# Two seven-product pairs in block 1 of a linear-attention and GEGLU kernel, and k-v of batch 1 on column halves

## The chip, the cores and the metric

The kernel runs on one core of a Trainium2 chip. The metric is the device time of one execution in microseconds (us), as the median of five runs. The engines are TensorE (PE, with its weight loads PEld), VectorE (DVE), ScalarE (ACT), GpSimd (POOL) and SyncE (SP), which issues nearly all of the transfers.

## The reference

For q, k and v of 8 batches, 8 heads, 576 positions and 64 values per head, it computes a linear attention: a softmax of q over the 64 values, a softmax of k over the 576 positions, kv = k-softmax transposed times v (64 x 64 per head), and x = q-softmax times kv. With the heads side by side, x is a matrix of 4608 rows and 512 columns. Then comes a GEGLU layer with 1536 inner columns:

```
kv  = einsum('bhsd,bhse->bhde', softmax(k, axis=2), v)
x   = einsum('bhsd,bhde->bhse', softmax(q, axis=-1), kv)   # -> [4608, 512]
g   = x @ w_gate
out = (0.5 * g * (1 + erf(g / sqrt(2))) * (x @ w_val)) @ w_out
```

## The kernel before, in words

**Blocks.** The work goes by batches. Each of the 8 batches has 512 main positions, which make one block of the layer; the 64 remaining positions of all batches make a ninth block, which is run before the last batch. While TensorE does the layer of batch b, the other engines prepare the attention of batch b + 1 and load batch b + 2 or so. There is no scheduler: every instruction stands where the program calls it, and side work is hung on places in the block with `at(b, kind, place, functions)` and called by `ride`. The kinds are FI (behind an inner tile of a block that is done tile by tile), PR (a letter in a written list of steps) and NS (places in the output stage).

**The layer, tile by tile.** The 1536 inner columns are 12 tiles of 128, numbered 0 to 11. A tile in its plain form is 4 matmuls of 512 columns for the gate (bank psg) and 4 for the value (psv), line 467. `gate` (line 470) then takes the Gelu on ScalarE into gl and multiplies on VectorE into ht, the inner activations. Blocks 0 and 1 do all twelve tiles like this. Their first tiles are interleaved with the end of the attention (`ffn_first0`, `ffn_first`), since the four parts of x arrive one by one.

**The layer, by seven products.** From block 2 on, the tiles k and k + 3 (k = 0, 1, 2, and 6, 7, 8 in some blocks) can be done as a pair by Strassen's seven products of half size instead of eight. `pair_step` (line 630) has four steps, written "k.1" to "k.4" in the lists: step 1 does products 1 and 5, step 2 products 6 and 3, step 3 products 7 and 2, step 4 product 4. Each product is 4 matmuls of 256 columns (line 606), so a pair is 28. In between, ScalarE copies bank pga to pgb and takes snapshots (snq), VectorE adds them into a tile cc or into the idle eq buffer of odd batches (cc_b), ScalarE takes the Gelu of cc, and GpSimd multiplies its halves into ht (`upper`, line 653). It needs sums of the weights (`sum_wgv`, tiles ws and, in place, wg_sb and wv_sb) and four sums of x (`sum_x`, GpSimd, line 593, tile xs). The lists THREE (block 2), FOUR and SIX (lines 611 to 616) give the order of the steps; "6g" and "6v" are the gate and the value half of plain tile 6 (`half`, line 620), the letters are places for side work.

**The output.** Blocks from 1 on use seven products again in `out_strassen` (line 728): products 1, 2, 5, 6, 3, 7, 4 of 12 matmuls each (line 718), in banks psa, psb, psc. They need sums of ht (`sum_h`, line 566: s1 and s2 in sh, one in place in ht, one in s4) and of the output weights (`sum_w`, line 552, tiles tw). In block 1 all of the ht sums are on VectorE, in steps of two neighbouring tiles (SUMS, line 706); in later blocks a part of them is on GpSimd, in steps of tiles j, j + 3, j + 6 and j + 9.

**The attention.** `exp` (line 208, ScalarE) makes eq and ek; `norm` or `norm_pair` (lines 235 and 253) reduce on VectorE and multiply on GpSimd or VectorE; `cast_v` (line 217) casts v on GpSimd; k-v is `unit_kv` for batch 1 (`kv_mm`, line 279: 10 matmuls of 130 columns for two head pairs, of which the mask keeps the diagonal blocks) and `unit_kv4` from batch 2 on (line 336: 40 matmuls of 65 columns, two heads on the two column halves). q is transposed by TensorE for batches 0 and 1, and by one transfer for batch 2 on (`unit_td`, line 383, issued by SyncE). `unit_x` and `unit_x4` make x. ek and v have one buffer each, eq has two.

**Places around the change.** In block 1 the eq of batch 2 is normalized behind tiles 2 to 4 (tile numbers 0-based), the first half of its k is exponentiated behind tile 4, its v is cast behind tile 5 and its q transposed behind tile 8. The second half of k and the q of batch 3 are exponentiated behind tile 11, the k of batch 3 in the output stage after `unit_kv4` of batch 2; there v of batch 3 is loaded and cast too. `unit_x4` of batch 2 comes before the last product, and then `one_ring` joins the two banks kept for the attention (att_ring) with the other six.

## Time and profile before

| | us |
|---|---|
| median of five runs | 293.68 (293.62 to 293.84) |
| the profiled execution | 293.66 |
| its span in the profile | 291.9 |
| TensorE busy | 282.5 |
| VectorE busy | 222.2 |
| GpSimd busy | 200.5 |
| ScalarE busy | 194.9 |
| block 1 on TensorE, first matmul of its first tile to the first of block 2 | 48.59 to 81.73 |
| output stage of block 1 | 70.76 to 81.73 |
| block 2 to its output stage | 81.73 to 101.27 |

The clock granted to TensorE was full over the whole span. In the views of the profile, a row of the order of work gives the start in us from the start of the span, the duration in us, the engine, the line of the program, the operation, what it writes from what it reads, the shape, how many instructions are merged in the row, and in brackets the idle time before it with the releaser. Matmul rows overlap at their ends, as each matmul is shown until its result is out. "PE pskv L343" is TensorE's write to tile pskv at line 343. SPq is SyncE's queue, whose rows show how long the queue was held by issuing, not how long a transfer took.

### The profile page before, as it was taken

The numbers are of one execution on the slowest core, as the hardware profiler recorded it, in microseconds if no ns is written. First come the engines' busy times: TensorE is split into PE (matmuls) and PEld (weight loads), VectorE is DVE, ScalarE is ACT, GpSimd is POOL, SyncE is SP. The second block draws the span as 40 slices with busy tenths as digits, with TensorE's granted clock in tenths as the row PEclk, the third lists the DMA queues.
The fourth block names the chain that finished last, engine by engine and source line by source line (L and its number), as shares of the span: only waits on it lengthen the run. The fifth ranks groups of instructions, "written<-read, shape, count | busy, mean of one in ns | idle before, by whom it ended". The sixth has DMA issues, their size and how long they took to land.

```text
span 291.9 us, 6352 instructions
## 1 busy us (share of the span) xinstructions
PE 282.5 (97%) x2449; PEld 203.0 (70%) x2449; DVE 222.2 (76%) x412; ACT 194.9 (67%) x322; POOL 200.5 (69%) x187
## 2 busy tenths in 40 slices
PE   3999999999999999999999999999999999999994
PEld 1444445445866687778776878687868888888883
DVE  2954889878878768677967797687868879938992
ACT  3763367785786578758986798669864577537650
POOL 1557746970489799877888688869895576283640
PEclk9999999999999999999999999999999999999999
DMA  6999999998059704990299119901141110033003
GB/s 216 374 381 387 401 392 390 357 342 236 5 183 380 158 3 144 352 225 3 116 313 277 36 74 325 323 3 74 73 78 25 72 74 0 3 72 75 0 2 144
DMA packets 54622, 51.72 MB, mean 177 GB/s; under 512 B 18496, under 2 KB 50496, under 8 KB 54592
## 3 DMA queue, kind: packets, MB, share of 16 engines
q1 hardware_dynamic: 52864, 49.49, 53.9%
q10 hardware_dynamic: 1728, 1.84, 1.9%
q8 instruction: 19, 0.31, 0.5%
q14 instruction: 11, 0.09, 0.1%
HBM read 37.75 MB, written 9.44 MB: 162 GB/s over the span
## 4 chain that ended last, share of the span: by engine, by line
PE 94%; DVE 2%; DMA 2%; ACT 0%; issue 0%; ACTq 0%
PE pga L606 19%; PE psa L718 15%; PE psg L467 14%; PE psv L467 14%; PE pgc L606 9%; PE psc L718 7%; PE pgb L606 5%; PE psb L718 4%; PE psy L535 4%; DMA qt<-in_q_dram 2%; PE pskv L343 2%; PE psx L430 1%; DVE rq L240 1%; PE psx L409 1%; DVE eq L250 0%; PE pskv L284 0%
## 5 line engine op out<-in xcount | busy, mean ns | idle before, releaser
L467 PE MATMUL psg<-xt,wg_sb 128*128 128x512 f16 x184 | 49.3, 379 | 0.0
L467 PE MATMUL psv<-xt,wv_sb 128*128 128x512 f16 x184 | 49.2, 379 | 0.0
L250 POOL TENSOR_TENSOR eq<-eq,rrq 128x640 f16<-128x640 f16 (+1 forms) x27 | 34.7, 1305 | 11.6 <-DVE rrq L242 8.1
L718 PEld LDWEIGHTS <-ht 128*128 128x128 f16 x384 | 36.6, 98 | 7.6 <-issue 2.5
L606 PEld LDWEIGHTS <-wv_sb 128*128 128x128 f16 x248 | 24.1, 98 | 9.4 <-issue 1.0
L467 PEld LDWEIGHTS <-wv_sb 128*128 128x128 f16 x184 | 17.9, 98 | 18.0 <-issue 0.2
L653 POOL TENSOR_TENSOR ht<-eq 128x512 f16<-128x512 f32 x14 | 17.8, 1272 | 18.0 <-ACT eq L651 18.0
L467 PEld LDWEIGHTS <-wg_sb 128*128 128x128 f16 x184 | 18.0, 98 | 16.5
L576 POOL TENSOR_TENSOR s<-ht,sh 128x512 f16<-128x512 f16 x19 | 22.4, 1178 | 9.8 <-DVE sh L576 9.8
L634 DVE SCALAR_TENSOR_TENSOR ht<-pga,glq 128x256 f16<-128x256 f32 x31 | 13.1, 421 | 20.7 <-ACT glq L633 20.6
L188 POOL CAST v<-vt 128x640 f16<-128x640 f32 x26 | 18.8, 763 | 12.8 <-PE pskv L343 11.3
L576 POOL TENSOR_TENSOR ht<-ht 128x512 f16<-128x512 f16 x19 | 23.1, 1216 | 6.1 <-DVE sh L576 6.1
L606 PEld LDWEIGHTS <-wg_sb 128*128 128x128 f16 x248 | 24.2, 98 | 2.8
L653 POOL TENSOR_TENSOR ht<-cc 128x512 f16<-128x512 f32 x15 | 19.5, 1302 | 8.5 <-ACT cc L651 8.5
L472 ACT ACTIVATE gl<-psg 128x512 f32<-128x512 f32 x24 | 13.8, 598 | 16.6 <-PE psg L467 16.5
L633 ACT ACTIVATE glq<-pgb 128x256 f32<-128x256 f32 x31 | 11.7, 379 | 18.7 <-PE pgb L606 10.9
L718 PE MATMUL psa<-tw,ht 128*128 128x256 f16 x192 | 23.4, 272 | 0.1
L473 DVE SCALAR_TENSOR_TENSOR ht<-psv,gl 128x512 f16<-128x512 f32 x24 | 16.1, 686 | 9.3 <-PE psv L467 7.4
L212 ACT ACTIVATE ek<-kt 128x1280 f16<-128x1280 f32 (+1 forms) x11 | 19.1, 1748 | 5.5 <-DMA kt<-in_k_dram 4.0
L663 ACT COPY pgb<-pga 128x512 f32<-128x512 f32 x31 | 18.0, 580 | 6.7 <-PE pga L606 6.4
L643 ACT ACTIVATE snq<-pga 128x512 f32<-128x512 f32 x31 | 18.5, 599 | 4.0 <-PE pga L606 3.7
L240 DVE TENSOR_REDUCE rq<-eq 128x20 f32<-128x1280 f16 (+1 forms) x12 | 17.2, 1431 | 4.5 <-ACT eq L212 4.5
(172 smaller groups left out, 729.2 us busy)
## 6 DMA issues: line engine op xcount, KB each, us to landing
out_dram<-yo SPq DMA_DIRECT2D x15, 512.0 KB, 3.4
kt<-in_k_dram SPq DMA_DIRECT2D x7, 640.0 KB, 9.5
vt<-in_v_dram SPq DMA_DIRECT2D x7, 640.0 KB, 5.6
qt<-in_q_dram SPq DMA_DIRECT2D x7, 640.0 KB, 8.1
qt<-in_q_dram SPq DMA_DIRECT2D x8, 512.0 KB, 8.2
wost<-in_moe_w_out_dram SPq DMA_DIRECT2D x6, 512.0 KB, 7.9
kt<-in_k_dram SPq DMA_DIRECT2D x6, 512.0 KB, 9.3
vt<-in_v_dram SPq DMA_DIRECT2D x6, 512.0 KB, 6.0
```

The source lines that it names most:

```text
L188: nc.gpsimd.tensor_copy(out=dst, in_=src)
L212: nc.scalar.activation(out=dst[:, n0:NC, h0 * D:h1 * D].rearrange(o, d=D, **({"t": 2} if b >= QUAD else {})), in_=heads(tiles[(nm, b)], b, ...
L240: nc.vector.reduce_sum(rq, e, axis=mybir.AxisListType.X)
L250: (nc.gpsimd if eng == "pool" else nc.vector).tensor_tensor(out=e, in0=e, in1=rrq.unsqueeze(-1).to_broadcast((P, n, 2, D)), op=ALU.mult)
L467: nc.tensor.matmul(ps, w[:, ci, fi * P:(fi + 1) * P], xt[:, ci, :], start=(ci == 0), stop=(ci == HP - 1))
L473: nc.vector.scalar_tensor_tensor(out=ht[:, fi, :], in0=psv, scalar=_H_SCALE, in1=gl, op0=ALU.mult, op1=ALU.mult)
L576: (nc.gpsimd if eng == "pool" else nc.vector).tensor_tensor(out=o, in0=a, in1=b, op=op)
L606: nc.tensor.matmul(ps[:, t], a, x, start=(first and t == 0 and c == 0), stop=(c == 1), skip_group_check=True)
L643: nc.scalar.activation(out=sn, in_=ps, func=ACTF.Copy, scale=_H_SCALE)
L653: (nc.vector if k == NFI - NO // 2 - 1 else nc.gpsimd).tensor_tensor(out=ht[:, k:k + NO // 2 + 1:NO // 2, 256:512], in0=cc[:, :, 0], in1=c ...
L663: nc.scalar.copy(out=pb, in_=pa)
L718: nc.tensor.matmul(ps[t], a, w, start=(first and j == js[0] and (t == ts[0] or ps[t].tensor is not ps[ts[0]].tensor)), stop=(j == js[-1]), ...
```

## The change

Block 1 gets a list of steps of its own, TWO. Its first three tiles, interleaved with the end of the attention, are now 6, 7 and 8; then come tile 9, two pairs in turns (0 with 3, 1 with 4), and tiles 10, 11, 2 and 5 in the plain form. The sums of x of batch 1 and the normalization of batch 2 in pairs go behind tile 8; the second of the two rings is joined right after the first three tiles. The weight sums that pairs 0 and 1 need in place of wg_sb and wv_sb (`sum_wgv` 3) are made in block 0, those of pair 2 stay in block 1. The ht sums of block 1 go as in later blocks: steps of j, j + 3, j + 6, j + 9, half of them on GpSimd, except those of the last step. The whole k of batch 2 is exponentiated at the end of the block's first output product ("e"), followed by q of batch 3. v of batch 2 is cast in two halves (at "c", before the pairs, and at "d", behind them); its q is normalized at "n" and "m" and its transpose issued at "t", behind step 1.4. The k-v of batch 1 is made like that of batch 2, with two heads on the two column halves.

```diff
-    def kv_mm(b, g, j):
...
-    def kv_norm(b, g):
...
     def unit_kv(b, g):
-        kv_mm(b, g, 0)
-        kv_mm(b, g, 1)
-        kv_norm(b, g)
+        ps = small([P, 2, VW], f32, "pskv")
+        for j in range(2):
+            hp = 2 * g + j
+            for n in range(NC):
+                for s in range(2):
+                    c0 = hp * P + s * D
+                    nc.tensor.matmul(
+                        ps[s * D:(s + 1) * D, j, :], ek_b[0][:, n, c0:c0 + D],
+                        v16_b[0][:, n, 2 * hp + s, 0:VW], start=(n == 0), stop=(n == NC - 1))
+        rck = att.tile([P, 2], f32, name="rck", tag="rck")
+        nc.vector.reciprocal(out=rck, in_=ps[:, :, D])
+        for j in range(2):
+            kv_sb = att.tile([P, 2, D], f16, name="kv_sb", tag="kv", bufs=8)
+            nc.vector.scalar_tensor_tensor(
+                out=kv_sb, in0=ps[:, j, 0:D].unsqueeze(1).to_broadcast((P, 2, D)),
+                scalar=rck[:, j:j + 1], in1=mask, op0=ALU.mult, op1=ALU.mult)
+            st[(b, "kv", 2 * g + j)] = kv_sb
...
-    def ffn_first(xt, after):
+    def ffn_first(xt, f0, after):
...
     def sum_h(j0, j1, which, eng="dve"):
-        step = 1 if j1 - j0 == 2 else NO // 2
+        step = NO // 2
...
+    TWO = ("l 9g 9v n c 0.1 1.1 0.2 1.2 0.3 1.3 m d 10g 0.4 1.4 w 10v t 11g s0 11v u0 2g s1 2v u1 5g 5v")
...
-            live["odd"] = odd = b > 2 and not live.get("odd", True)
+            live["odd"] = odd = b != 2 and not live.get("odd", True)
...
-    SUMS = {7: (0, 2, (1, 2)), 8: (0, 2, (3, 4)), 9: (2, 4, (1, 2)), 10: (2, 4, (3, 4))}
...
-        js = (0, 1, 2, 3, 4, 5) if b < 2 else (0, 3, 1, 4, 2, 5)
+        js, late = (0, 3, 1, 4, 2, 5), NO // 2 - 1
...
-              [L(unit_x, 1, 3, "dve"), L(norm, 2, 0, "pool"), L(norm, 2, 1, "pool")]]
+              [L(unit_x, 1, 3, "dve"), lambda: sum_x(get_x(1)), L(norm_pair, 2, 0, 0, ("pool", "pool"))]]
...
-    at(1, FI, 2, L(unit_trem, 1))
-    at(1, FI, 3, L(norm, 2, 2, "pool"), L(load_batch, 3, ((q, "q"), (k, "k"))))
-    at(1, FI, 4, L(exp, "k", 2, 0, 4), L(norm, 2, 3, "pool"), L(sum_w, 4), make_s)
-    at(1, FI, 5, L(cast_v, 2, 0, H))
-    at(1, FI, 8, L(unit_td, 2))
-    at(1, FI, 11, L(exp, "k", 2, 4, 8), L(exp, "q", 3))
-    at(1, NS, 2, L(unit_kv4, 2), L(exp, "k", 3), L(load_batch, 3, ((v, "v"),)), L(cast_v, 3, 0, H))
-    at(1, NS, 4, L(unit_x4, 2, ("act", "dve"), 1), one_ring, L(preload, ACTF.Gelu),
-       lambda: sum_x(get_x(2)))
...
-    at(0, FI, NFI - 2, L(sum_w, 1))
-    at(1, NS, 1, L(sum_wgv, "g", 3))
-    at(1, NS, 2, L(sum_wgv, "v", 3))
+    at(0, FI, 8, L(sum_wgv, "g", 3, 0, 2))
+    at(0, FI, 9, L(sum_wgv, "v", 3, 0, 2))
+    at(0, FI, 10, L(sum_w, 1))
+    at(1, FI, 1, L(unit_trem, 1))
+    at(1, PR, "l", L(load_batch, 3, ((q, "q"), (k, "k"))))
+    at(1, PR, "n", L(norm_pair, 2, 1, 0, ()))
+    at(1, PR, "c", L(cast_v, 2, 0, 4))
+    at(1, PR, "m", L(norm_mul, 2, 2, "pool"), L(norm_mul, 2, 3, "pool"))
+    at(1, PR, "d", L(cast_v, 2, 4, H))
+    at(1, PR, "w", L(sum_w, 4), make_s)
+    at(1, PR, "t", L(unit_td, 2))
+    at(1, PR, "e", L(exp, "k", 2, 0, 4), L(exp, "k", 2, 4, 8), L(exp, "q", 3))
+    at(1, NS, 1, L(sum_wgv, "g", 3, 2, 1))
+    at(1, NS, 2, L(unit_kv4, 2), L(exp, "k", 3), L(load_batch, 3, ((v, "v"),)), L(cast_v, 3, 0, H),
+       L(sum_wgv, "v", 3, 2, 1))
+    at(1, NS, 4, L(unit_x4, 2, ("act", "dve"), 1), L(preload, ACTF.Gelu), lambda: sum_x(get_x(2)))
...
-    for b in range(2, B + 1):
+    for b in range(1, B + 1):
         for j in range(NO // 2 - 1):
             at(b, PR, f"s{j}", L(sum_h, j, NO, (1,)))
...
-                ffn_first(xt, first1)
-            fi0 = 2 if b == 0 else 3
+                ffn_first(xt, NO, first1)
+                one_ring()
+            fi0 = 2
             ride(b, FI, fi0 - 1)
-        if b > 1:
+        if b > 0:
             go_on(b, xt)
-        for fi in range(fi0, NFI if b < 2 else 0):
-            ffn_fi(xt, fi, b == 1 and fi == 7)
+        for fi in range(fi0, NFI if b == 0 else 0):
+            ffn_fi(xt, fi)
             ride(b, FI, fi)
-            if b > 0 and fi in SUMS:
-                sum_h(*SUMS[fi])
```

## The prediction

> **What bounds the kernel now.** I read the page's busy shares and chain first, then TensorE's order of work through block 1, then the order of work of GpSimd, SyncE and VectorE from block 1 into block 2. The page:
>
> ```profile
> PE 282.5 (97%) x2449; PEld 203.0 (70%) x2449; DVE 222.2 (76%) x412; ACT 194.9 (67%) x322; POOL 200.5 (69%) x187
> PE 94%; DVE 2%; DMA 2%; ACT 0%; issue 0%; ACTq 0%
> ```
>
> TensorE is the chain from about 20 us on, so less TensorE work is less time, if nothing else then comes late. TensorE's order of work in block 1 and at the start of block 2:
>
> ```profile
> 49.90 0.74 PE L284 MATMUL pskv<-v,ek 128*128 128x130 f16 x10
> 55.22 1.03 PE L467 MATMUL psg<-xt,wg_sb 128*128 128x512 f16 x4
> 56.09 1.03 PE L467 MATMUL psv<-xt,wv_sb 128*128 128x512 f16 x4
> ...
> 76.10 0.82 PE L343 MATMUL pskv<-v,ek 128*64 128x65 f16 x40
> ...
> 83.46 0.38 PE L606 MATMUL pga<-xt,wv_sb 128*128 128x256 f16 x2
> 83.68 0.38 PE L606 MATMUL pga<-xt,wg_sb 128*128 128x256 f16 x2
> 83.90 0.38 PE L606 MATMUL pgc<-xs,wsv 128*128 128x256 f16 x2
> ```
>
> Rows overlap at their ends, so prices come from the distance between starts. Four 512-column matmuls take 0.865 us (55.22 to 56.09); two of 256 take 0.218 (83.46 to 83.68); the ten matmuls of a k-v pair 0.58 (49.90 to 50.48); the forty half-width ones about 0.75 (76.10 to 76.85, where the next row starts). No gap is in sight between 50.48 and 81.73.
>
> The side that can come late is GpSimd and the loads that it waits for:
>
> ```profile
> 52.42 3.10 POOL L557 TENSOR_TENSOR tw<-wo_sb,tw 128x1536 f16<-128x1536 f16 x1
> 60.70 1.89 POOL L250 TENSOR_TENSOR eq<-eq,rrq 128x640 f16<-128x640 f16 x1 [0.40 <-DVE rrq L232]
> 62.53 2.71 POOL L188 CAST v<-vt 128x640 f16<-128x640 f32 x4
> 76.58 3.04 POOL L188 CAST v<-vt 128x640 f16<-128x640 f32 x4 [11.33 <-PE pskv L343]
> 81.56 1.16 POOL L593 TENSOR_TENSOR xs<-xt 128x512 f16<-128x512 f16 x1 [1.94 <-ACT xt L190]
> 91.08 1.27 POOL L653 TENSOR_TENSOR ht<-cc 128x512 f16<-128x512 f32 x1
> ```
>
> ```profile
> 62.61 4.39 SPq L386 DMA_TRANSPOSE eqt<-eq  x1
> 67.10 1.29 SPq L168 DMA_DIRECT2D vt<-in_v_dram  x2
> ```
>
> SyncE issues the transpose of batch 2's q the moment GpSimd's last normalization ends (60.70 + 1.89 = 62.59), and only then v of batch 3. GpSimd idles 11.33 us before the casts of batch 3, which wait for TensorE's k-v of batch 2. From 81.56 to 91.08 it runs without a gap into the product that frees tile cc. VectorE writes cc again here, and TensorE's seventh product of that pair follows:
>
> ```profile
> 92.47 0.68 DVE L647 SCALAR_TENSOR_TENSOR cc<-pgc,snq 128x512 f32<-128x512 f32 x1
> 93.22 0.69 DVE L647 SCALAR_TENSOR_TENSOR cc<-pga,snq 128x512 f32<-128x512 f32 x1
> ```
>
> GpSimd leaves cc at 92.35, 0.12 before VectorE's write. VectorE ends the second at 93.91; step 1.4's product, which overwrites the bank that it read, starts at 94.32.
>
> **What the skill says.** "TensorEngine Tiling (Array Packing)", Performance Considerations: a stationary side of up to 64 columns can run as two column tiles, up to twice as fast. The trace agrees less than fully: 0.375 us for twenty half-width matmuls (half of 0.75) against 0.58 for ten full ones. "DMA: Bandwidth & Descriptors", Queues, rings and completion order: SyncE has one ring per DMA engine, consumed in order; so v of batch 3 stays behind the transpose, as the rows at 62.61 and 67.10 show. "SBUF — State Buffer", Who interferes with whom: GpSimd and a VectorE instruction with two SBUF inputs exclude each other; hence the spread of the same cast, 2.71 against 3.04 for four. "ScalarE: Activation LUTs", What ACT_TABLE_LOAD costs: 1283 ns and a drain of 1380; the trace has the 1.28 and no drain (a Gelu ends at 58.61, the load starts at 58.63, the Exp at 59.92).
>
> **The change, part by part.** (1) Two pairs by seven products. A pair is 28 matmuls of 256 columns, 28 x 0.109 = 3.05 us, where the two tiles that it replaces are sixteen matmuls of 512 columns, 16/4 x 0.865 = 3.46. Gain 0.41 a pair, 0.81 in all (unrounded), on the path.
>
> (2) k-v on column halves: 0.58 - 0.375 = 0.2 for each of two. But VectorE is busy without a pause from 46.41 to 51.52 (reciprocals, kv_sb, the normalization of batch 1, an eviction, a transposed copy), and the x matmul at 51.34 needs its kv_sb, which I put at about 51.25. VectorE itself moves at most by its 0.14 pause before 46.41 and the like. I take 0.17 of the 0.4; bounds 0.05 and 0.4. Sum: 0.98 us less TensorE work that can show.
>
> (3) The four weight sums moved into block 0 are two VectorE instructions of about 0.4 us, between gates that leave it 0.3 to 0.6 idle each; two shorter ones stay. Cost nothing; without the cover under 0.4.
>
> (4) k2's exp. Its first half leaves ScalarE's middle, with two table loads of 1.28, and goes to the end beside the other half, the q3 and the k3 exps. New end order: last Gelu near 69.7, table load to 71.0, two halves to 73.5 (1.27 and 1.18), q3 to 75.8 (2.32). TensorE wants ek for batch 2's k-v at 76.10 - 0.98 = 75.1, so 1.6 to spare; k3's exp waits for that k-v as before. Cost nothing; if that cover were gone, up to one half's 1.3.
>
> (5) Inside block 1 the pairs need xs by GpSimd, snapshots by ScalarE, additions by VectorE. Batch 3's block already runs the same order ("n 0.1 6.1 0.2 6.2 0.3 6.3 m 10g") without a gap over 0.1 us in TensorE's rows from 113.97 to 125. There xs is ready 1.2 us before its product; here GpSimd's weight sum ends at 55.47, the first xs at 56.65, and its product starts at 56.8 + 0.44 = 57.2: 0.6 to spare. The odd pair writes the eq buffer that the transpose of batch 1's remainder reads (issued at 50.97, landing 8.6 later: 59.6); VectorE gets there near 60.8. Two paired reductions (1.47 and 0.28 each, row at 82.25) replace four single ones (0.81 and 0.22), and merging the two bank rings early gives this block the eight banks that batch 3's has. Cost 0 to 0.3, taken as 0.05.
>
> (6) GpSimd's queue, the part that decides. From 55.47: four xs sums 4.57 (81.56 to 86.13), two normalizations 2.44 (86.13 to 88.57), two casts of v 1.36 (half of 2.71), two cc products 2.46 (119.90 to 122.36), two normalizations 2.48: 68.78. The transpose of batch 2 is issued there, 6.2 us later than now (the loads of q and k for batch 3 stand ahead of it on SyncE as before). Its own reader is not near: it lands 4.9 to 7.2 after issue, by 76.0, and TensorE takes it at 78.6. But behind it on SyncE stands v of batch 3. The transpose holds the queue 3.36 to 4.39 us; the loads of q and k for batch 3, now beside it, will be over, so I take 3.5: 72.28. The second v transfer is issued 0.65 later and lands 5.9 after (5.8 to 6.1): 78.83. Meanwhile GpSimd has two casts and, new there, four ht sums (4 x 1.2) and is free by about 75.0; TensorE wants the last of these sums near 76.2. Now the casts waited until 76.58, for TensorE; then they wait for this load. Four casts, 2.71 to 3.11, taken as 2.8: 81.63, when batch 2's xs sums can start. Now they start at 81.56. So GpSimd comes out in place (+0.07), while TensorE wants to come 0.93 us earlier.
>
> What is late next: the first xs is done at 82.8, wanted at 83.90 - 0.93 = 82.97, just in time. The cc product is not: cc free at 92.35 + 0.07, VectorE's two additions end at 92.5 + 0.61 + 0.69 = 93.8, and step 1.4, with 0.08 of hand-over, starts at 93.87 instead of 94.32. So 0.45 us of the 0.93 survive and 0.48 are lost in block 2. After that GpSimd idles 1.72 us before 100.55 on ScalarE, so the lateness ends there, but TensorE's lost time stays lost. Profiled execution: span 291.9 - 0.45 = 291.45, with 1.76 around it 293.2; the profiled run's 293.66 stands 0.02 below the median of 293.68, so the same on the median.
>
> The bounds of (6): transpose 3.36, load 5.8, casts 2.71 give xs at 81.30 and a gain of 0.78; 4.39, 6.1 and 3.11 give 83.03 and a loss of 0.95.
>
> **The rivals.** Nothing waits: the whole 0.93 stays, 292.7. For it: the cc margin is built from ends of rows, and the load may run quicker on a quiet queue. Against it: GpSimd has no slack from 81.56 to 92.35. Slower: v of batch 3 lands late because GpSimd's chain stretches (six more instructions ahead of the transpose, beside VectorE) or the transpose holds SyncE as long as now. The place is the same, step 1.4 of block 2; TensorE's shift is the xs shift minus 0.52, so it turns into a loss once the xs sums start after 82.1, and is beyond 0.2% from 82.7 on. At 83.0: 294.6; I take 294.4 for it. A third: the pairs of block 1 stall by themselves (tight banks, 0.14 us between VectorE's last ht of tile 5 and its product): about 0.5 more, 293.6.
>
> **How the numbers follow.** 0.2% of 293.68 is 0.59 us, about what a measurement of this kernel can tell from no change. Half-eaten gain (292.9 to 293.7): 0.48; about a third of it lies beyond 0.59. Nothing waits: 0.25. Slower by late v: 0.18. Stalls within block 1: 0.09, without a visible difference. Faster 0.25 + 0.17 = 0.42; same 0.31 + 0.09 = 0.40; slower 0.18. The range, 292.6 to 294.3, leaves out under 0.1 at each end; the likeliest case's own is 292.9 to 293.7.
>
> **What would show it.** Right: transpose issue of batch 2 at 68.5 to 69.3 on SyncE, v of batch 3 at 72 to 73, its casts waiting on DMA and not on TensorE until about 78.8, xs sums at 81.3 to 82.1; TensorE about 0.95 early at the end of block 1 and a gap before step 1.4 of block 2. A gap at the first or second pair in block 1 would show (5) wrong; a ScalarE exp that ends after 75.1 would show (4) wrong; x of batch 1 not moving at all would show (2) wrong. The prediction fails upward if v lands after 80, downward if it lands by 78.

## The result, and the profile after

The changed kernel takes 294.47 us (median; 294.2 to 294.7) against 293.69 of the kernel before on the same chips: 1.0025 times, with a 95% interval of 1.0019 to 1.0031. That is 0.78 us slower, and clear of the 0.59 us (0.2%) that the prediction took for what can be told from no change; forecast were 293.2, with 292.6 to 294.3 as the range. The profiled execution took 294.44, its span is 292.7 (291.9 before).

The page of the changed kernel, the line that answers to the one of before:

```profile
PE 282.2 (96%) x2493; PEld 205.0 (70%) x2493; DVE 225.4 (77%) x410; ACT 195.3 (67%) x328; POOL 212.4 (73%) x197
```

TensorE has less to do, as forecast for the pairs, but GpSimd has 11.9 us more. VectorE is busy 3.2 us longer although it has two instructions fewer (410 for 412), so on average they are longer. The two lists differ in their instructions too; the rows below show where it matters.

In the kernel before, the first two output products of block 1 followed each other without a gap:

```profile
70.76 1.47 PE L718 MATMUL psa<-wo_sb,ht 128*128 128x256 f16 x12
72.07 1.47 PE L718 MATMUL psb<-wo_sb,ht 128*128 128x256 f16 x12
```

TensorE's order of work through the end of block 1 in the changed kernel (its line numbers are about 9 to 12 lower: L458 is a plain tile, L597 a pair, L709 an output product, L334 the k-v of batch 2):

```profile
55.26 1.03 PE L458 MATMUL psg<-xt,wg_sb 128*128 128x512 f16 x4
...
70.00 1.04 PE L709 MATMUL psa<-wo_sb,ht 128*128 128x256 f16 x8
71.43 0.39 PE L709 MATMUL psa<-wo_sb,ht 128*128 128x256 f16 x2 [0.39 <-DVE ht L620]
72.36 0.39 PE L709 MATMUL psa<-wo_sb,ht 128*128 128x256 f16 x2 [0.54 <-DVE ht L620]
72.59 1.47 PE L709 MATMUL psb<-wo_sb,ht 128*128 128x256 f16 x12
...
76.61 0.82 PE L334 MATMUL pskv<-v,ek 128*64 128x65 f16 x40
77.70 1.47 PE L709 MATMUL psc<-wo_sb,s 128*128 128x256 f16 x12 [0.26 <-DVE sn L738]
...
82.56 1.03 PE L458 MATMUL psg<-xt,wg_sb 128*128 128x512 f16 x4
```

Up to 70.00 all goes as forecast: the output stage begins 0.76 us earlier than before (70.76), that is the 0.80 of the pairs less a start of tile 9 that is 0.04 later. Then the gain is spent at once. Product 1 waits twice for `DVE ht L620`, the gates of tiles 2 and 5, and takes 72.59 - 70.00 = 2.59 us; before, the same twelve matmuls took 1.31. That is 1.28 lost. Between the k-v and product 3 it loses 0.34 more (76.61 to 77.70 is 1.09, where it takes 0.75 without a gap). Together that is 1.62 by the rounded rows; the whole output stage is 1.59 longer (12.56 for 10.97). Less the 0.76 gained ahead of it that makes 0.83: block 2 starts at 82.56 instead of 81.73. From there the shift stays as it is: step 1.4's product in block 2 starts at 95.15 (94.32 before) and the output stage of block 2 at 102.09 (101.27 before).

Why are the gates late? First VectorE's rows in the kernel before (L557 is the sum of the output weights into tw, L576 a sum of ht), in which the gates (L473) take 0.68 or 0.69:

```profile
60.53 0.93 DVE L557 TENSOR_TENSOR tw<-wo_sb,tw 128x1536 f16<-128x1536 f16 x1
...
65.06 0.46 DVE L576 TENSOR_TENSOR sh<-ht 128x512 f16<-128x512 f16 x1
65.55 0.42 DVE L576 TENSOR_TENSOR sh<-sh,ht 128x512 f16<-128x512 f16 x1
...
66.49 0.41 DVE L576 TENSOR_TENSOR ht<-ht 128x512 f16<-128x512 f16 x1
```

Now the changed kernel (tw is L548, a sum of ht L567, the gate of a tile in the list of steps L620):

```profile
65.33 1.78 DVE L548 TENSOR_TENSOR tw<-wo_sb,tw 128x1536 f16<-128x1536 f16 x1
67.03 0.68 DVE L620 SCALAR_TENSOR_TENSOR ht<-psv,gl 128x512 f16<-128x512 f32 x1
67.63 0.88 DVE L567 TENSOR_TENSOR sh<-ht 128x512 f16<-128x512 f16 x1
68.43 0.68 DVE L620 SCALAR_TENSOR_TENSOR ht<-psv,gl 128x512 f16<-128x512 f32 x1
69.03 0.88 DVE L567 TENSOR_TENSOR sh<-sh,ht 128x512 f16<-128x512 f16 x1
69.84 0.93 DVE L567 TENSOR_TENSOR sh<-ht 128x512 f16<-128x512 f16 x1
70.69 0.68 DVE L620 SCALAR_TENSOR_TENSOR ht<-psv,gl 128x512 f16<-128x512 f32 x1
71.29 0.41 DVE L567 TENSOR_TENSOR sh<-sh,ht 128x512 f16<-128x512 f16 x1
71.62 0.68 DVE L620 SCALAR_TENSOR_TENSOR ht<-psv,gl 128x512 f16<-128x512 f32 x1
```

From 65.33 to 72.30 VectorE has no pause. The gates take 0.68 each, as they did before. The sums of ht (same shape and type) took 0.41 to 0.46 in block 1 of the kernel before; here three of the four ahead of the last gate take 0.88 to 0.93. The tw sum took 0.93 and takes 1.78. An estimate from these rows: without the excess, 0.85 + 0.47 + 0.47 + 0.52 = 2.31 us, the last gate would not be held by VectorE's list at all (72.30 - 2.31 = 70.0, and its own tile's matmuls end at 70.17); it would be done near 70.9, and product 1 wants it at 71.1 (ten matmuls of 0.109 after 70.00). The three of the later sums that are long too (1.26 at 73.03, 1.11 at 75.60, 0.66 at 72.34) delay the snapshot sn that product 3 waits for.

GpSimd's order of work beside it:

```profile
65.03 1.27 POOL L646 TENSOR_TENSOR ht<-eq 128x512 f16<-128x512 f32 x1
66.25 3.38 POOL L250 TENSOR_TENSOR eq<-eq,rrq 128x640 f16<-128x640 f16 x2
69.58 1.77 POOL L188 CAST v<-vt 128x640 f16<-128x640 f32 x2
71.31 1.40 POOL L567 TENSOR_TENSOR ht<-ht 128x512 f16<-128x512 f16 x1
...
79.39 2.71 POOL L188 CAST v<-vt 128x640 f16<-128x640 f32 x4 [2.96 <-DMA vt<-in_v_dram]
```

In the kernel before GpSimd was idle from 65.24 to 76.58, while VectorE made its sums (65.06 to 74.94). Now it works through the whole of it, and its instructions are long as well: two normalizations 3.38 (2.49 at 60.03), two casts 1.77 (1.38 at 62.46).

### The profile page after: what moved, and what is told of

It reads as the page before. It is cut to its first block, busy times and chain, and to the rows that moved or that the text cites. A ratio compares the mean times of both kernels' runs of the same rounds, so it can differ in the third digit from the quotient of the medians.

```text
span 292.7 us, 6450 instructions
## 1 busy us (share of the span) xinstructions
PE 282.2 (96%) x2493; PEld 205.0 (70%) x2493; DVE 225.4 (77%) x410; ACT 195.3 (67%) x328; POOL 212.4 (73%) x197
## 4 chain that ended last, share of the span: by engine, by line
PE 72%; DVE 1%; issue 0%
PE pga L597 19%; PE psa L709 14%; PE pgc L597 9%; PE psc L709 7%; PE psg L458 7%; PE psv L458 6%; PE pgb L597 5%; PE psb L709 3%; PE pskv L334 1%; PE psx L421 1%; PE psxr L421 0%; DVE s L567 0%; DVE yo L744 0%; DVE sn L738 0%; DVE yo L821 0%; DVE ht L567 0%
## 5 line engine op out<-in xcount | busy, mean ns | idle before, releaser
L458 PE MATMUL psg<-xt,wg_sb 128*128 128x512 f16 x168 | 45.2, 379 | 0.0
L458 PE MATMUL psv<-xt,wv_sb 128*128 128x512 f16 x168 | 45.1, 379 | 0.0
L709 PEld LDWEIGHTS <-ht 128*128 128x128 f16 x384 | 36.4, 98 | 9.0 <-issue 2.5
L597 PEld LDWEIGHTS <-wv_sb 128*128 128x128 f16 x264 | 25.6, 98 | 10.0 <-issue 1.0
L646 POOL TENSOR_TENSOR ht<-eq 128x512 f16<-128x512 f32 x15 | 19.1, 1271 | 18.0 <-ACT eq L644 18.0
L567 POOL TENSOR_TENSOR s<-ht,sh 128x512 f16<-128x512 f16 x21 | 24.8, 1183 | 9.8 <-DVE sh L567 9.8
L567 POOL TENSOR_TENSOR ht<-ht 128x512 f16<-128x512 f16 x21 | 25.8, 1230 | 6.2 <-DVE sh L567 6.2
L597 PEld LDWEIGHTS <-wg_sb 128*128 128x128 f16 x264 | 25.8, 98 | 3.0
L458 PEld LDWEIGHTS <-wv_sb 128*128 128x128 f16 x168 | 16.3, 98 | 15.9 <-issue 0.5
L646 POOL TENSOR_TENSOR ht<-cc 128x512 f16<-128x512 f32 x16 | 20.8, 1299 | 8.5 <-ACT cc L644 8.5
L458 PEld LDWEIGHTS <-wg_sb 128*128 128x128 f16 x168 | 16.3, 98 | 14.4
L626 ACT ACTIVATE glq<-pgb 128x256 f32<-128x256 f32 x33 | 12.5, 378 | 19.8 <-PE pgb L597 11.9
L656 ACT COPY pgb<-pga 128x512 f32<-128x512 f32 x33 | 19.2, 581 | 7.4 <-PE pga L597 7.1
L240 DVE TENSOR_REDUCE rq<-eq 128x20 f32<-128x1280 f16 (+1 forms) x14 | 20.1, 1437 | 4.6 <-ACT eq L212 4.6
L709 PE MATMUL psa<-tw,ht 128*128 128x256 f16 x192 | 23.4, 272 | 0.1
L618 ACT ACTIVATE gl<-psg 128x512 f32<-128x512 f32 x27 | 16.0, 592 | 7.3 <-PE psg L458 7.3
L597 PE MATMUL pga<-xs,wg_sb 128*128 128x256 f16 x108 | 20.6, 272 | 0.0
```

Of the source, the lines that this page charges most:

```text
L240: nc.vector.reduce_sum(rq, e, axis=mybir.AxisListType.X)
L458: nc.tensor.matmul(ps, w[:, ci, fi * P:(fi + 1) * P], xt[:, ci, :], start=(ci == 0), stop=(ci == HP - 1))
L567: (nc.gpsimd if eng == "pool" else nc.vector).tensor_tensor(out=o, in0=a, in1=b, op=op)
L597: nc.tensor.matmul(ps[:, t], a, x, start=(first and t == 0 and c == 0), stop=(c == 1), skip_group_check=True)
L618: nc.scalar.activation(out=live[c], in_=t, func=ACTF.Gelu)
L646: (nc.vector if k == NFI - NO // 2 - 1 else nc.gpsimd).tensor_tensor(out=ht[:, k:k + NO // 2 + 1:NO // 2, 256:512], in0=cc[:, :, 0], in1=c ...
```

## The experiments

**Theory C (exclusion).** A VectorE instruction with two inputs in SBUF and a GpSimd instruction that reads SBUF can't run at once; the change put GpSimd's work beside VectorE's sums, these wait, the gates behind them come late, and TensorE stands. The Trainium skill says this in "SBUF — State Buffer", Who interferes with whom and Summary: rules for kernel authors: where VectorE has two SBUF inputs and GpSimd reads SBUF, the second to issue "fully blocks" until the first finishes; a VectorE instruction with at most one SBUF input, outside its two-port modes, doesn't contend, which fits the gates (one input in PSUM, 0.63 to 0.69 in every run, with GpSimd beside them or not). **Theory O (order).** VectorE's list in this stage is simply too long or in the wrong order, whatever GpSimd does. **A third**, the prediction's own slower case, v of batch 3 coming late into block 2, is out already by the trace: no wait at step 1.4.

All runs in one table. The ratio is to the runs of the kernel before that stood beside each (medians of 293.64 for e1 to e4, 293.69 for the rest). In e1 and e8 a part of the work is left out. "Product 1" is from its start to the start of product 2 (1.31 without a gap), "output stage" from the start of product 1 to block 2, both on TensorE in the profiled execution.

| run | median us | ratio to before (95%) | product 1 | output stage |
|---|---|---|---|---|
| before | 293.69 | | 1.31 | 10.97 |
| changed | 294.47 | 1.0025 (1.0019 to 1.0031) | 2.59 | 12.56 |
| e1, GpSimd quieter (work left out) | 293.56 | 0.9999 (0.9990 to 1.0007) | 1.91 | 11.58 |
| e2, tw earlier | 294.35 | 1.0023 (1.0014 to 1.0032) | 1.82 | 12.48 |
| e3, gates first | 297.65 | 1.0129 (1.0101 to 1.0156) | 1.31 | 15.80 |
| e4, k-v alone | 293.63 | 1.0001 (0.9993 to 1.0009) | 1.31 | 10.97 |
| e5, v on ScalarE | 293.81 | 1.0012 (1.0005 to 1.0019) | 2.31 | 11.97 |
| e6, sums on VectorE | 294.25 | 1.0017 (1.0009 to 1.0026) | 2.80 | 12.46 |
| e7, both and v first | 293.52 | 0.9992 (0.9984 to 1.0000) | 1.98 | 11.76 |
| e8, no overlap (work left out) | 293.00 | 0.9986 (0.9968 to 1.0003) | 1.31 | 11.09 |
| e9, e7 with gates first | 294.69 | 1.0034 (1.0022 to 1.0046) | 1.31 | 12.84 |
| e10, exp in the middle | 297.13 | 1.0103 (1.0076 to 1.0130) | 3.96 | 15.16 |
| e11, before, cast later | 293.69 | 1.0001 (0.9993 to 1.0009) | 1.31 | 10.97 |
| e12, v cast whole | 295.36 | 1.0078 (1.0056 to 1.0100) | 3.83 | 13.49 |
| e13, e9 with the cast held | 293.21 | 0.9984 (0.9977 to 0.9990) | 1.31 | 11.30 |

**e1: GpSimd's work beside the sums left out.** The edits are against the changed kernel where nothing else is said.

```diff
-    at(1, PR, "m", L(norm_mul, 2, 2, "pool"), L(norm_mul, 2, 3, "pool"))
-    at(1, PR, "d", L(cast_v, 2, 4, H))
```

> The changed kernel without two things that GpSimd does while VectorE makes the ht sums of block 1: the multiplications that normalize the upper four heads of batch 2's q, and the casts of the upper half of its v (so batch 2 is computed from wrong values). VectorE's list is untouched. Theory C (the two engines exclude each other): the tw sum falls from 1.78 to about 0.93 us, the first sums of ht from 0.88 to 0.93 us to 0.41 to 0.5, the gap in output product 1 of block 1 goes from 1.28 to below 0.2, and the median falls to 292.8 to 293.2. Theory O (the order: too much stands ahead of the last two ht tiles on VectorE, whatever it costs): a gap of 0.5 or more stays, 293.6 to 294.0.

0.9 us come back, but Theory C's numbers were missed: product 1 still takes 1.91, a wait of 0.60 where C allowed 0.2, and with 293.56 the run lies where Theory O had it (a wait of 0.5 or more, 293.6 to 294.0). The rows show why: the tw sum (1.62) still meets the two upper combinations, and the later sums now meet GpSimd's own sums of ht, which start earlier (0.99, 0.78 and 1.26 beside them, 0.41 where GpSimd is idle). The overlap was only half taken away, and e1 alone doesn't decide.

**e2: the weight sum ahead.**

```diff
-    at(1, PR, "d", L(cast_v, 2, 4, H))
-    at(1, PR, "w", L(sum_w, 4), make_s)
+    at(1, PR, "d", L(cast_v, 2, 4, H), L(sum_w, 4))
+    at(1, PR, "w", make_s)
```

> The changed kernel with the sum of the output weights for product 4 (tw, 1.78 us on VectorE) called before tile 10 instead of behind step 1.4, where VectorE idles 1.05 us for ScalarE. VectorE's overhang at the last ht tiles was about 1.3 to 2.4 us. Theory C: the sum costs about twice its own time wherever GpSimd is busy, so taking it away removes 1.0 to 1.8 us of the queue; gap in product 1 down from 1.28 to 0 to 0.4, median 293.3 to 293.8. Theory O: only its undisturbed 0.9 us counts; gap 0.3 to 0.5, median 293.6 to 293.9. If neither, and the pairs' own additions are pushed by it, TensorE loses 0.5 or more in the pairs instead.

Theory C's number was missed, and Theory O's as well. The tw sum fell to 1.03 and product 1 lost only 0.5, but VectorE, being earlier, met GpSimd's upper combination and normalizations with more of its sums (1.27, 0.88, 1.48, then 1.35 and 1.26), and products 6 and 3 waited for the snapshots, 0.27 and 0.52. To order VectorE differently moves the collision; it doesn't remove it. This alone doesn't decide either.

**e3: the gates of tiles 2 and 5 ahead of the sums.**

```diff
-... w 10v t 11g s0 11v u0 2g s1 2v u1 5g 5v")
+... w 10v t 11g 11v 2g 2v s0 5g 5v u0 s1 u1")
```

> The changed kernel with the ht sums behind the gate products on VectorE: end of the list 11g 11v 2g 2v s0 5g 5v u0 s1 u1. Both theories: no gap in product 1. Theory C: the sums still take twice their time and now come late for products 5 and 6, so 0.3 to 0.9 us of the 1.28 come back there; median 293.5 to 294.1. Theory O: nothing waits later; median 292.9 to 293.3. My prediction's own point, v of batch 3 behind the transpose, should be seen next in either case: a wait of TensorE at step 1.4 of block 2 or at its first xs product.

Worse than either theory said. Product 1 has no gap any more, but the sums come all together, and GpSimd's sums of ht beside them. VectorE of this run:

```profile
71.46 1.37 DVE L567 TENSOR_TENSOR sh<-ht 128x512 f16<-128x512 f16 x1
72.87 1.26 DVE L567 TENSOR_TENSOR sh<-sh,ht 128x512 f16<-128x512 f16 x1
74.05 1.37 DVE L567 TENSOR_TENSOR sh<-ht 128x512 f16<-128x512 f16 x1
75.46 1.26 DVE L567 TENSOR_TENSOR sh<-sh,ht 128x512 f16<-128x512 f16 x1
```

GpSimd of this run:

```profile
71.23 1.32 POOL L567 TENSOR_TENSOR ht<-ht 128x512 f16<-128x512 f16 x1
72.52 1.33 POOL L567 TENSOR_TENSOR s<-ht,sh 128x512 f16<-128x512 f16 x1
73.81 1.33 POOL L567 TENSOR_TENSOR ht<-ht 128x512 f16<-128x512 f16 x1
75.11 1.33 POOL L567 TENSOR_TENSOR s<-ht,sh 128x512 f16<-128x512 f16 x1
```

The two engines go in lockstep, one instruction each per 1.3 us: a sum of 0.41 costs VectorE three times its price. And each waits for the other's end: the four sums of VectorE end at 72.83, 74.13, 75.42 and 76.72, each 0.28 after the end of the GpSimd instruction beside it (72.55, 73.85, 75.14, 76.44), and GpSimd's last three end 1.01 to 1.02 after the end of VectorE's. Two instructions that shared a rate would not end at such fixed distances.

The same distance stands everywhere. In the traces of all fifteen kernels 229 sums of ht of this shape on VectorE take over 0.5 us, and every one of them ends 0.27 to 0.29 after the end of a GpSimd instruction; the other 613 take 0.40 to 0.48. In the changed kernel it is so for each of the three long sums ahead of the last gate.

Product 5 waits for the sums, product 6 next:

```profile
75.48 0.61 PE L709 MATMUL psc<-tw,sh 128*128 128x256 f16 x4 [1.74 <-DVE sh L567]
77.37 2.72 PE L709 MATMUL psa<-tw,sh 128*128 128x256 f16 x12 [1.28 <-DVE sn L738]
```

**e4: the k-v on column halves alone**: the kernel before with `unit_kv` of the change (the diff of that function above, nothing else).

> The kernel before with nothing but k-v of batch 1 on column halves. If VectorE's chain holds x of batch 1, as the prediction has it: 0.05 to 0.2 us faster, 293.5 to 293.65, and k-v matmuls of about 0.44 us for 20 instead of 0.58 for 10. Rival: TensorE's whole saving of 0.28 to 0.4 us is kept, 293.3 to 293.4.

No measurable difference, and the same starts on TensorE as before from 70.76 on. Twenty half-width matmuls take 0.44 instead of 0.58, but the first of them starts 0.54 after the transposes ahead of it instead of 0.45, and the x matmul starts when VectorE's kv_sb is done, at 51.32 (51.34 before). So VectorE's chain does hold x, and the 0.05 to 0.2 us of the expectation didn't come.

**e5: the second half of v of batch 2 on ScalarE**, behind "11g" and "2g" in two pieces, and the tw sum at "d".

```diff
-... w 10v t 11g s0 11v u0 2g s1 2v u1 5g 5v")
+... w 10v t 11g f s0 11v u0 2g h s1 2v u1 5g 5v")
...
-    at(1, PR, "d", L(cast_v, 2, 4, H))
-    at(1, PR, "w", L(sum_w, 4), make_s)
+    at(1, PR, "d", L(sum_w, 4))
+    at(1, PR, "f", L(cast_v, 2, 4, 6, "act"))
+    at(1, PR, "h", L(cast_v, 2, 6, H, "act"))
+    at(1, PR, "w", make_s)
```

> The changed kernel with tw before tile 10 (as in the run e2) and the casts of the upper half of batch 2's v on ScalarE, which idles 1.1 us behind each of the last Gelus, instead of on GpSimd. Theory C (VectorE's sums of two SBUF operands wait for the end of a GpSimd instruction and back): GpSimd is quiet 1.8 us earlier, but its ht sums still meet VectorE's; the gaps of TensorE in output products 1 and 3, 1.6 in all in the changed kernel, shrink to 0.7 to 1.2; median 293.7 to 294.2. Theory O (too much on VectorE, whoever else runs): as e2, 294.3 to 294.5, since VectorE's list is e2's.

0.66 us better than the changed kernel, as Theory C had it. Product 1 keeps a wait of 0.82; the sums ahead of it still take 1.39, 0.88 and 1.48 beside the upper combination and the normalizations.

**e6: GpSimd's four sums of ht of block 1 given to VectorE**, in the output stage.

```diff
-    at(1, NS, 1, L(sum_wgv, "g", 3, 2, 1))
+    at(1, NS, 1, L(sum_h, 0, NO, (4,)), L(sum_h, 1, NO, (4,)), L(sum_h, 0, NO, (3,)), L(sum_h, 1, NO, (3,)),
+       L(sum_wgv, "g", 3, 2, 1))
...
-            if j and b >= B - 1:
+            if b == 1:
+                at(b, PR, f"u{j}", L(sum_h, j, NO, (2,)))
+            elif j and b >= B - 1:
```

> The changed kernel with the four ht sums of block 1 that went to GpSimd (for products 7 and 3) on VectorE, behind its second snapshot in the output stage. VectorE gets four instructions more, GpSimd four fewer. Theory C: the sums beside them fall to 0.41 to 0.5 us from 71 us on, but tw and the first sums still meet the normalization and the casts; gaps 0.5 to 1.2 in all, median 293.6 to 294.2. Theory O: VectorE has 1.7 us more to do before products 3 and 7, so the gaps grow: 294.8 to 296.

VectorE gets four instructions more, and yet its sums after 71.6 fall to 0.41 to 0.43 and the later products don't wait any more. The sums ahead of product 1, beside the normalizations and the cast, stay long (0.88, 0.88, 0.93; tw 1.99), and so does product 1. Each group of sums follows what GpSimd does beside it. The time hardly moves, though: 294.25 is 0.05 above Theory C's range, and its interval overlaps that of the changed kernel; it is far below the 294.8 at least of Theory O.

**e7: e5 and e6 together, and the load of v of batch 3 ahead of the transpose on SyncE**, both behind "2g". Beside the diffs of e5 and e6:

```diff
-... w 10v t 11g f s0 11v u0 2g h s1 2v u1 5g 5v")
+... w 10v 11g f s0 11v u0 2g h t s1 2v u1 5g 5v")
...
-    at(1, PR, "t", L(unit_td, 2))
+    at(1, PR, "t", L(load_batch, 3, ((v, "v"),)), L(unit_td, 2))
...
-    at(1, NS, 2, L(unit_kv4, 2), L(exp, "k", 3), L(load_batch, 3, ((v, "v"),)), L(cast_v, 3, 0, H),
+    at(1, NS, 2, L(unit_kv4, 2), L(exp, "k", 3), L(cast_v, 3, 0, H),
```

> Both of these and, so that v of batch 3 isn't late, its load ahead of batch 2's transpose on SyncE. Theory C: only the two normalizations of batch 2 meet VectorE's sums; gaps 0 to 0.5 in all, TensorE 0.3 to 0.8 us ahead of the kernel before at the start of block 2, and no wait of GpSimd for v; median 292.9 to 293.4, which would beat both kernels. Theory O: 294.3 or more.

The first version with all of the change and nothing left out that isn't slower than before; Theory C's 293.4 at most was missed by 0.12. What is left is 0.67 us in product 1, again with sums of 1.42, 0.88 and 1.48 beside GpSimd's upper combination and normalizations.

**e8: no overlap with the sums of ht**: the edits of e1, e2 (without its cast) and e6 together.

> The run e1 (two normalizations and the upper casts of v of batch 2 left out, so batch 2 is computed from wrong values) with tw before tile 10 and all of block 1's ht sums on VectorE: nothing of GpSimd's runs beside VectorE's sums. Theory C: each sum 0.41 to 0.5 us, no gap of TensorE in block 1's output stage over 0.1, the pairs' 0.8 us kept whole: 292.7 to 293.0. Theory O: VectorE's list is the longest of all variants, so the gaps stay at 0.6 or more: 293.6 or more.

VectorE's rows, and the first two output products on TensorE:

```profile
67.02 0.41 DVE L567 TENSOR_TENSOR sh<-ht 128x512 f16<-128x512 f16 x1
...
67.96 0.41 DVE L567 TENSOR_TENSOR sh<-sh,ht 128x512 f16<-128x512 f16 x1
68.29 0.41 DVE L567 TENSOR_TENSOR sh<-ht 128x512 f16<-128x512 f16 x1
```

```profile
70.34 1.47 PE L709 MATMUL psa<-wo_sb,ht 128*128 128x256 f16 x12
71.65 1.47 PE L709 MATMUL psb<-wo_sb,ht 128*128 128x256 f16 x12
```

VectorE has as long a list in this stage as any run, every sum of ht takes 0.41 to 0.43 (GpSimd is idle from 66.98 to 76.15), and product 1 has no gap. Theory O, which says the opposite, falls as the cause; the order still decides where a long sum hurts, as e2 and e3 show. (The tw sum, beside the upper combinations, takes 1.98, but ahead of everything.) The output stage is at 11.09, within 0.12 of before, and from tile 9 to the output stage TensorE needs 14.75 (15.54 before), so the pairs' 0.8 is kept there. This profiled execution had come to tile 9 0.37 late, so block 2 starts only 0.31 earlier than before. The median is 293.00, but one of the ten executions took 295.82, and the interval of the ratio just reaches 1.

**e11: the kernel before, with only the cast moved.** A copy of two columns of ht holds GpSimd's cast of v of batch 2 until tile 7's gate is done.

```diff
-    at(1, FI, 5, L(cast_v, 2, 0, H))
+    def hold():
+        t = att.tile([P, 2], f16, name="hold", tag="hold", bufs=1)
+        nc.gpsimd.tensor_copy(out=t, in_=ht[:, 7, 0:2])
+
+    at(1, FI, 7, hold, L(cast_v, 2, 0, H))
```

> The kernel before, in which GpSimd's cast of v of batch 2 waits (through a copy of two columns of ht) for tile 7's product, so that it starts near 65 us, where VectorE's sums of ht start, instead of at 62.5. Nothing else differs and nothing is left out. Theory C: the sums of ht that lie beside the cast (four or five, 65.1 to 67.8 us) take 0.7 us or more instead of 0.41 to 0.46 and the later ones stay at 0.41; the cast takes longer than its 2.71 us. The end doesn't move (293.5 to 293.9), since VectorE has idle time there before each later tile. Theory O: the sums stay at 0.41 to 0.46 wherever the cast lies.

The cleanest of all: but for the small copy, no other instruction differs. VectorE of this run, with the cast at 65.57 to 68.9 on GpSimd:

```profile
65.16 0.43 DVE L576 TENSOR_TENSOR sh<-ht 128x512 f16<-128x512 f16 x1
65.62 0.95 DVE L576 TENSOR_TENSOR sh<-sh,ht 128x512 f16<-128x512 f16 x1
66.48 0.68 DVE L473 SCALAR_TENSOR_TENSOR ht<-psv,gl 128x512 f16<-128x512 f32 x1
67.09 0.41 DVE L576 TENSOR_TENSOR ht<-ht 128x512 f16<-128x512 f16 x1
67.42 0.93 DVE L576 TENSOR_TENSOR s<-ht,sh 128x512 f16<-128x512 f16 x1
...
68.98 0.42 DVE L576 TENSOR_TENSOR sh<-ht 128x512 f16<-128x512 f16 x1
```

GpSimd of this run:

```profile
65.57 3.36 POOL L188 CAST v<-vt 128x640 f16<-128x640 f32 x4
```

Two sums, not the four or five expected, take more than double; a third (67.09) came just ahead of a cast, which then waited for it, and the four casts take 3.36 instead of 2.71. One by one, the first cast runs from 65.57 to 66.28 and the sum of 65.62 ends at 66.56; the third cast ends at 68.08 and the sum of 67.42 at 68.35: 0.28 and 0.27 after the cast, the distance of e3. The last three casts in turn end 0.58 after the end of a sum each. So it is no sharing of a rate: one waits until the other's instruction is over, as the skill says, and which of the two waits changes from meeting to meeting. The time doesn't move, since here VectorE has pauses.

**e9: e7 with the gates first**, now that GpSimd has nothing beside most of the sums.

```diff
-... w 10v 11g f s0 11v u0 2g h t s1 2v u1 5g 5v")
+... w 10v 11g f 11v 2g h t 2v s0 5g 5v u0 s1 u1")
```

> The relieved kernel (v of batch 2 partly cast by ScalarE, the eight sums of ht of block 1 all on VectorE, v of batch 3 loaded ahead of the transpose), and in it the products of the gates of tiles 2 and 5 put ahead of the sums of ht on VectorE, as in the run with the gates first. Nothing of the computation is left out. Theory C (exclusion by GpSimd): the gates-first order failed only because the sums behind it ran in lockstep with GpSimd's sums; GpSimd now has nothing there, so the sums take 0.41 to 0.43 us and product 1 starts and goes on without a gap (the relieved kernel lost about 0.6 us there): 292.9 to 293.3 us, 0.9975 to 0.9990 of before. Theory O (VectorE simply has too much to do in the stage): the wait comes back at product 5, as it did with the gates first, and the time is 293.8 us or more.

Theory C's time was missed by 1.4 us, and the time is one that Theory O allowed, though not with its wait (product 5). Products 1, 2, 5 and 6 follow without a gap. Then product 7 waits:

```profile
79.18 1.47 PE L709 MATMUL psa<-tw,ht 128*128 128x256 f16 x12 [1.71 <-DVE sn L738]
```

VectorE of this run shows a pair of sums of 1.79 just ahead, which took 0.75 in e7:

```profile
75.35 0.75 DVE L567 TENSOR_TENSOR s<-ht,sh 128x512 f16<-128x512 f16 x2
76.02 1.79 DVE L567 TENSOR_TENSOR ht<-ht 128x512 f16<-128x512 f16 x2
```

TensorE was now so early that its k-v of batch 2 released the cast of v of batch 3 at 75.71 (76.42 in e7), on top of those sums. The faster engine had moved GpSimd's work into the next collision. So far this is an argument from one trace; e13 tries it.

**e13: e9 with that cast held** behind VectorE's last sum of ht, by the same kind of copy.

```diff
+    def hold():
+        t = att.tile([P, 2], f16, name="hold", tag="hold", bufs=1)
+        nc.gpsimd.tensor_copy(out=t, in_=ht[:, 1, 256:258])
+
-    at(1, NS, 2, L(unit_kv4, 2), L(exp, "k", 3), L(cast_v, 3, 0, H),
+    at(1, NS, 2, L(unit_kv4, 2), L(exp, "k", 3), hold, L(cast_v, 3, 0, H),
```

> The run before it with the gates first in the relieved kernel, and one thing more: GpSimd's cast of v of batch 3 waits (through a copy of two columns of ht) for VectorE's last sum of ht, so that it starts near 77 us instead of at 75.7 and doesn't lie beside the sums of 75.3 to 77.8. Nothing is left out. Theory C (exclusion): the wait of 1.71 us at product 7 came from a pair of sums that took 1.79 us beside this cast instead of 0.75; with the cast held the pair takes 0.75 again, the wait falls to 0.7 us or less, and the time to 292.8 to 293.6, below before. Theory O (the order on VectorE, whatever GpSimd does): with the gates first the sums are simply due too late, the wait at product 7 stays above 1.4 us, and the time at 294.4 to 294.8.

VectorE's list is e9's, and the pair of sums is back at 0.75:

```profile
75.28 0.75 DVE L567 TENSOR_TENSOR s<-ht,sh 128x512 f16<-128x512 f16 x2
75.94 0.75 DVE L567 TENSOR_TENSOR ht<-ht 128x512 f16<-128x512 f16 x2
```

The wait at product 7 falls from 1.71 to 0.16, block 2 starts at 81.12 (e9: 82.74) and the kernel takes 293.21: 0.48 us faster than before, 1.26 faster than the change as it was made. The 0.48 are less than 0.2%, but the interval of the ratio (0.9977 to 0.9990) leaves 1 out. The wait in e9 was the cast beside the sums, not the order; for this wait that settles between C and O.

**e10 and e12: two other parts of the change undone.** The first diff is e10's, the second e12's.

```diff
-    at(1, PR, "w", L(sum_w, 4), make_s)
-    at(1, PR, "e", L(exp, "k", 2, 0, 4), L(exp, "k", 2, 4, 8), L(exp, "q", 3))
+    at(1, PR, "w", L(sum_w, 4), make_s, L(exp, "k", 2, 0, 4))
+    at(1, PR, "e", L(exp, "k", 2, 4, 8), L(exp, "q", 3))
```

```diff
-    at(1, PR, "c", L(cast_v, 2, 0, 4))
-    at(1, PR, "d", L(cast_v, 2, 4, H))
+    at(1, PR, "c", L(cast_v, 2, 0, H))
```

> The changed kernel with the first half of k2's exp put back into the middle of block 1 (behind the sums of wo, between tiles 10 and 11), at the price of two more loads of ScalarE's table; nothing is left out. The prediction's step on the exp (moving it to the end costs nothing) and theory C: at best nothing changes, 294.3 to 294.6; where ScalarE's gelu of tile 10 or 11 comes later through the exp (1.2 us and two table loads) and TensorE's products wait for it, up to 295.0. If instead the exp at the end were a cause of the loss, this run would be near 293.7.

> The changed kernel with v of batch 2 cast in one piece, where its first half was (ahead of the two upper combinations on GpSimd), instead of in halves; nothing is left out. Theory C: the second half's 1.35 us goes out of the stage of the sums, but the upper combinations come 1.3 to 1.8 us later, and the pair's products with them; if these have that much in hand, the sums beside the cast's old place (69.6 to 71.4 us) fall to 0.41 and the time falls to 293.9 to 294.3; if not, TensorE waits at the second pair and the time is 294.5 to 295.5. If GpSimd's work has no part in the loss, 294.4 as the changed kernel.

Both make it worse. In e10 the exp and its table loads push tile 11's Gelu from 65.89 to 68.78, and the next two behind it, and the gates with them; its expectation of 295.0 at most was missed. In e12 the cast pushes the upper combinations back by 1.4, with the normalizations behind them, and more sums meet them (tw 2.10, then 0.89, 0.88, 1.48). So the exp's move to the end and the cast in halves were right in themselves, worth about 0.8 us each in this order, by the executions at full clock (295.30 and 295.33 in e10, 295.13 to 295.40 in e12, against 294.47), and more where the clock fell, see the end.

## Why the prediction was wrong

**Step (1), the pairs, was right**: 0.81 forecast, 0.80 measured up to the output stage, without a gap at the pairs. **Step (2), k-v on column halves, gave nothing**: 0.17 forecast, 0.05 to 0.4 allowed. The x matmul starts at 51.36 (51.34 before), and tile 9 0.04 later, not earlier; by the prediction's own sign, x not moving at all, the step was wrong. The twenty matmuls take 0.44 (not 0.375) and start 0.09 later behind the transposes, and VectorE holds x as it did; e4, with this part alone, gives nothing measurable. That is 0.17 us of the error, not its cause. **Step (4), the exp, was right**: the q of batch 3 ended at 75.9 (75.8 forecast), no wait followed, and e10 shows the alternative to be worse.

**Step (5) failed, and with it the sign.** It said "Cost 0 to 0.3, taken as 0.05" for the pairs inside block 1. It asked after the waits of the pairs themselves, where it was right, and took every duration of VectorE from a kernel in which GpSimd was idle during the sums. The real cost came just behind the pairs: 1.28 us in product 1 and 0.34 ahead of product 3, 1.62 in all where 0.05 was taken. The rival "the pairs of block 1 stall by themselves" named the right spot, the short margin "between VectorE's last ht of tile 5 and its product", but gave it 0.5 us and a chance of 0.09, since it had no mechanism for it.

**Step (6) held the missing term.** It laid out GpSimd's new queue step by step, down to the normalizations, the casts and "four ht sums" between 66 and 75, and asked only when GpSimd would be done. It had even quoted the exclusion from the skill, and used it for nothing but the spread of GpSimd's cast. The other side of the same sentence, what VectorE pays, is the loss: four instructions ahead of the last gate took 2.31 us more than their price. One line that the prediction shows already had such a meeting in the kernel before: the normalization of 60.70 takes 1.89, where one alone takes 1.26, and VectorE's tw sum runs beside its start, from 60.53 to 61.46; there GpSimd paid. And the blocks that already share the sums with GpSimd have long sums in the kernel before too, eleven in all (1.26 at 134.6 in batch 3's block), but TensorE waits for none of them. So batch 3's block, which step (5) took as its model, showed that the order can run without a gap, not that VectorE's durations stay. e8 (no overlap: no wait at product 1), e11 (overlap alone: 0.42 becomes 0.95) and e13 against e9 (only a cast moved: 1.48 us of time) show the cause, and so do the fixed ends of the long sums (e3).

**The rest of step (6) can't be judged at its end.** The transpose was issued at 69.66 (68.78 forecast), v of batch 3 at 72.77 (72.28), its casts began at 79.39 (78.83) after a wait on the DMA, all 0.5 to 0.9 late, since GpSimd's instructions had stretched too. The predicted wait at step 1.4 of block 2 didn't come up, because TensorE itself came 0.83 later. Whether it would have stood there without the stall, no run shows: in e7, e9 and e13 the load of v was moved ahead, and e1 and e8 left out work ahead of it. An estimate from the rows of the changed kernel leaves it open. There the casts end at 82.10, GpSimd then waits only 0.3 for x, and VectorE's second addition, which step 1.4 needs, ends at 94.74. A TensorE without the 1.62 would have come to step 1.4 at 95.15 - 1.62 = 93.53. With GpSimd as late as it was, the addition could have ended only 0.3 earlier and TensorE would have waited 0.9; with GpSimd not stretched, and so 0.9 earlier, hardly at all. The 0.48 that step (6) took off in block 2 was not lost. That brought the forecast nearer to the result by luck: at the start of block 2 it was off by 1.76 us (0.93 earlier forecast, 0.83 later measured), on the median by 1.27.

**Step (3), the weight sums in block 0, cost little if anything**: tile 9 starts at 55.26, 0.04 later than before, which step (2) shares.

## What to carry to other kernels

When work is moved on GpSimd, lay its new span beside VectorE's instructions with two SBUF inputs and price every meeting on both sides: up to what is left of the GpSimd instruction on each sum and the other way round, and nothing on instructions like the gates, with one input in PSUM (0.63 to 0.69 in every run). A stage in which one of the two was idle is no source for durations of a stage in which both work. If such a stage can't be cleared, give the few sums to one engine (in e6, with four more sums on VectorE, the waits behind product 1 were gone, though the time hardly moved), and hold GpSimd's work by a real dependence where a faster engine would release it too early.

## What the runs showed of the hardware that was not expected

**Lockstep.** With both engines on sums of 128 x 512, one instruction on each takes about 1.3 us (e3), against 0.41 on VectorE and 1.15 on GpSimd alone. A sum of VectorE that met a GpSimd instruction ends 0.27 to 0.29 after that instruction, in all 229 cases of these traces.

**TensorE's clock after a short stall.** In e10 product 1 stood twice, for 1.27 and 0.90 us, and product 2 then took 2.56 us instead of 1.31. The windows of e10 (columns: window, its length, busy us of PE, PEld, DVE, ACT, POOL, granted clock, DMA share, GB/s):

```profile
70.00:74.00 4.00, 1.83 (x14) 1.10 (x13) 3.97 (x7) 3.97 (x4) 4.00 (x5) 0.96 0.82 155
74.00:78.00 4.00, 4.00 (x25) 2.94 (x24) 3.35 (x6) 1.17 (x1) 2.53 (x2) 0.61 0.87 261
```

The granted clock fell to 0.61 after the stall; of the six executions of e10 four took 297.1 to 298.2 and two 295.3. e3 has the same after 1.74 and 1.28 us (0.67 from 78 to 82), with three of its four executions at 297.5 to 298.5 and one at 295.96; this is a part of why both medians lie so high. e12's profiled execution stood as long (1.27 and 0.91) with the clock at 1.00 throughout, while two others of its six took 296.9 and 297.1 at a lower clock. "TensorE: Matmul & The Clock Gate", What's actually happening, gives a free-running activity window of about 3.4 us; no single gap here was that long, but two gaps close together came to 2.2 us and more. That would fit a window which is only sometimes mostly idle; no run was made to test it.
